# Causal score products of a complex linear-attention kernel: one 128-column product a head against two in 64-column tiles

## The chip, the cores and the metric

The kernel runs on one core of one Trainium2 chip. The metric is the device time of one execution in microseconds (us). The engines are named as in the profile: PE (TensorE, the matrix engine; PEld is its weight loads), DVE (VectorE), ACT (ScalarE), POOL (GpSimd) and SP (the queue that issues most transfers).

## What is computed

The reference is a recurrence over 768 time steps with a state of 48x48 complex numbers for each of 4 batches and 8 heads, and a mixture of experts behind it (cut here to what matters):

```
for t in range(S):                                  # attention
    new_re = ar * S_re - ai * S_im                  # ar, ai: decay of step t, one complex number a channel
    new_im = ar * S_im + ai * S_re
    S_re, S_im = new_re + k[t] v[t]^T, new_im
    y[t] = q[t] S_re
...
x = y of all heads, as rows of 384                  # experts
out[token] = sum over its 2 best of 8 experts of weight * relu(x @ w1[e]) @ w2[e]
```

## The kernel before, in words

The sequence is cut into chunks of 128 steps. A *unit* n is one batch and one chunk, 24 in all (6 chunks of 4 batches), with 8 heads each. Within a chunk the recurrence becomes a matrix product: with queries and keys turned and scaled by the accumulated decay, the output of a chunk is the masked scores times v, plus the queries times the state Z that came from the chunks before.

For a unit the kernel does this, by function and line of the profile:

- `p1`, `p2t`, `p2s`, `p3` (L286 to L344): logarithms, sums over the chunk on PE with a triangular matrix (L307, L331, tile `cum`), sines and exponentials on ACT, products on DVE. These fill `qh` and `kh`, the turned queries and keys.
- `tr_unit` (L354, L355): eight transposes on PE each of `qh` and `kh` into the PSUM tile `ptr`, which ACT copies to `qT` and `kT` (112 rows: 48 real, 16 empty, 48 imaginary).
- `sc_unit` (L363, L364), twice a unit with four heads each (a *half unit*, 48 in all): one product a head, keys as weights (128 columns) against 128 queries, into a quarter of the PSUM tile `psc`, of which there are two. DVE multiplies the four by the causal mask into `am`.
- `st_unit` (L374): 16 products of keys with v into `pG`, 48 columns wide; DVE adds `pG` to the state Z.
- `y_unit` (L412, L414): per head one product with Z and one with `am`, both 48 columns wide, into `pY`: even heads to partitions 0 to 47, odd heads to 64 to 111.
- `x_unit` (L427) and the gate (L436, 32 columns wide; L446; L477, L479) behind it, then scatter of the rows to the experts by POOL.

An fp32 product appears in the trace as two instructions (two passes), a transpose as one. A product of 48 columns in partitions 0 to 63 or 64 to 127 uses one half of the array's columns, and products in the two halves stand in the trace side by side.

What sets the order: a table of names written out by hand (`ORDER`, where P5a/P5b are the two half units of `sc_unit`, P6 `st_unit`, P7a/P7b `y_unit`, D12 the mask) fixes the order on PE, ACT and DVE for the first 17 of the 24 units; a list scheduler places the remaining units together with the first expert's weights (`load_w1`, `load_w2`), the first expert products (`mm1`, L684, which also use `psc`) and the gates. Transfers wait in SP's queue in program order; `load_v` (L267) of a unit stands behind the last reader of the buffer that it takes.

The experts follow (L684 `ph`, L734 `po`), from about 266 us on, and are not touched.

Of the kernel before, what the change touches and what calls it, by code (L numbers as in the profile page):

```python
# [9 lines left out]
F32 = mybir.dt.float32  # L10
# [5 lines left out]
OP = mybir.AluOpType  # L16
# [61 lines left out]
def kernel(  # L78
# [34 lines left out]
    def ones_where(t, cmp, pattern, cm, base, fill):  # L113
        nc.gpsimd.affine_select(out=t, in_=t, pattern=pattern, compare_op=cmp, fill=fill,
                                base=base, channel_multiplier=cm)
# [1 line left out]
    ident = cp.tile([128, 128], F32, name="ident")  # L117
    tri_t = cp.tile([128, 128], F32, name="tri_t")
    tri_l = cp.tile([128, 128], F32, name="tri_l")
    mask = cp.tile([128, 128], F32, name="mask")  # L120
    tri_b = cp.tile([128, 128], BF16, name="tri_b")
    ones_b = cp.tile([128, 128], BF16, name="ones_b")
    nc.vector.memset(tri_t, 1.0 / (2.0 * math.pi))
# [1 line left out]
    nc.vector.memset(tri_l, 0.25)  # L125
    ones_where(tri_l, OP.is_ge, [[1, 128]], -1, 0, -0.25)
    nc.vector.memset(mask, 1.0)
    ones_where(mask, OP.is_ge, [[1, 128]], -1, 0, 0.0)
    make_identity(nc, ident)
    nc.vector.memset(tri_b, 1.0)  # L130
    ones_where(tri_b, OP.is_gt, [[1, 128]], -1, 0, 0.0)
# [53 lines left out]
    nc.vector.memset(pG, 0.0)  # L185
    pY = psA.tile([128, H // 2, 128], F32, name="pY", bufs=1)
    nc.vector.memset(pY, 0.0)


    RE, IM, T0, TH, TF, TR, EE, QK, V = {}, {}, {}, {}, {}, {}, {}, {}, {}  # L190
# [49 lines left out]
    def key(name, ins):  # L240
        K.setdefault(name, []).append(ins)
        return ins
# [20 lines left out]
        nc.sync.dma_start(QK[n], qk[n])  # L263

    def load_v(n):
        V[n] = pa.tile([128, H, D], F32, name="v", bufs=6)
        nc.sync.dma_start(V[n].rearrange("p h d -> p (h d)"), v[n])  # L267

    def flat(t):
# [87 lines left out]
    def sc_unit(n, half):  # L357
        if half == 0:
            AM[n] = pa.tile([128, H, 128], F32, name="am", bufs=2)
        p = psA.tile([128, 4, 128], F32, name="psc")  # L360
        for j in range(4):
            h = 4 * half + j
            key(f"P5{'ab'[half]}.{n}", nc.tensor.matmul(p[:, j, :], KT[n][:, h, :], QT[n][:, h, :], start=True, stop=True))  # L363
        LAST['am'] = nc.vector.tensor_mul(AM[n][:, 4 * half:4 * half + 4, :], p, mask[:, None, :].to_broadcast([128, 4, 128]))  # L364
        key(f"D12{'ab'[half]}.{n}", LAST['am'])

    def st_unit(n):
# [31 lines left out]
    def y_unit(n, half):  # L399

        b, g = bt(n)
        if b == 0 and half == 0:
            XR[g] = pa.tile([128, B, ROW], F32, name="xr", bufs=3)
            nc.gpsimd.memset(XR[g][:, :, RNO + 1:ROW], 0.0)
            nc.gpsimd.tensor_copy(XR[g][:, :, RNO], tokid[:, g])
        for i in (2 * half, 2 * half + 1):
            for z in range(0 if g else 1, 2):
                for r in range(2):
                    h = 2 * i + r
                    o = pY[64 * r:64 * r + D, i, :]  # L410
                    if z == 0:
                        x = nc.tensor.matmul(o, Z[b][:, h, :], QT[n][:, h, :], start=True, stop=False, skip_group_check=True)  # L412
                    else:
                        x = nc.tensor.matmul(o, V[n][:, h, :], AM[n][:, h, :], start=not g, stop=True, skip_group_check=True)  # L414
                    key(f"P7{'ab'[half]}.{n}", x)
        if half == 0:
            return
        XT[n] = pa.tile([128, H // 2, 128], F32, name="xT", bufs=6)
        LAST['y'] = YC[n] = nc.scalar.activation(XT[n], pY, AF.Copy)
        key(f"A13.{n}", YC[n])  # L420
# [92 lines left out]
    def at(step, f, *a):  # L513
        fill.setdefault(step, []).append((f, a))
# [74 lines left out]
    def ps_tile(name, bufs=2):  # L589
        if psB and name == "px":  # L590
            return po_tile()
        if psB:
            return psB[0].tile([128, 512], F32, name=name, bufs=bufs)
        if name == "px":
            return psA.tile([128, H, 128], F32, name="ptr", bufs=1).rearrange("p a b -> p (a b)")[:, 0:512]
        return psA.tile([128, 4, 128], F32, name="psc").rearrange("p a b -> p (a b)")


    order = mybir.DependencyInfo(mybir.DependencyClass.NoSync, mybir.DependencyReason.DATA)
# [126 lines left out]
    def mm2_tile(e, w, j, p=None):  # L726
# [22 lines left out]
        if n == 128 and e in TAILS:  # L749

            for s in DONE.setdefault(e, []):
# [1 line left out]
            DONE[e].append(d)  # L753


    P = dict(la=10, p1=7, d1=1, p2=6, dt=0, ds=0, lqk=6, p3=4, d3=0, q=2, lv=5, xu=0.5, ss=3, gl=0, gd=0.25,
             tr=1.4, sc=-0.2, st=0.05, y=0.2, up=0.4, w1=16.5, w2=21.1, xt=17.8, m1=18.4, dm=0.36, xu1=22.8, w1b=23, co=6, hg=50,
             hx=50, hl=200, s0=(7, 5.5, 4.5), s1=(7.5, 6, 5), qd=0.05, tk=0.4, sh=0.05)
    pri = {gpick: P["hg"], gdis: P["hg"], gscat: P["hg"], x_unit: P["hx"], glog: P["hl"], gturn: P["hl"]}
# [26 lines left out]
            for i in range(2):  # L786
                at(pos(n + .5 - P["q"] + i * P["qd"], f"D{10 + i}.{n}"), p3q, n, i)
    for n in range(NT):
        at(-18.7 + .01 * n if n < 6 else behind_key(n + .5 - P["lv"], f"P7b.{n - 6}"), load_v, n)
        for i in range(2):  # L790
            at(pos(n - P["tr"] + P["tk"] * i, f"P{3 + i}.{n}"), tr_unit, n, i)
        for half in range(2):
# [149 lines left out]
    def slow_attention():  # L942
        with tc.tile_pool(name="sa", bufs=1) as sa, tc.tile_pool(name="sps", bufs=1, space=PSUM) as sps:
# [7 lines left out]
            with tc.For_i(0, NG, 1) as ci, tc.For_i(0, C, 1) as tt:  # L951
# [7 lines left out]
                        nc.sync.dma_start(x[:, 2 + i, b * H:(b + 1) * H],  # L959
                                          a6[bass.ds(ci, 1), bass.ds(tt, 1), i, :, b // 2, b % 2].rearrange("g s d h -> (g s d) h"))  # L960
                vb = sa.tile(sh, F32, name="vb")
                v4 = v.rearrange("(g b) s x -> g s b x", b=B)
                for b in range(B):
                    nc.sync.dma_start(vb[:, b * H:(b + 1) * H, :].rearrange("p h d -> p (h d)"),
                                      v4[bass.ds(ci, 1), bass.ds(tt, 1), b].rearrange("g s x -> (g s) x").to_broadcast([D, HD]))
# [109 lines left out]
def _laid_out(inputs, np):  # L1075

    x = {n: _tiles(np.asarray(inputs[n]), np) for n in ("q", "k", "v", "a_re", "a_im")}
    C, HD = x["q"].shape[1:]
    B = inputs["q"].shape[0]
    a = np.stack([x["a_re"].reshape(-1, 2, C, HD), x["a_im"].reshape(-1, 2, C, HD)], 1)  # L1080
    noise = np.asarray(inputs["moe_noise"])
    E = noise.shape[1]
    laid = dict(inputs, qk=np.stack([x["q"], x["k"]], 2), v=x["v"], a=a.transpose(0, 1, 3, 2, 4),
                moe_noise=noise.reshape(B, -1, C, E).transpose(2, 1, 0, 3).reshape(C, -1, E))
    return {n: laid[n] for n in _INS}

# [21 lines left out]
```

## Time and profile before

| | |
|---|---|
| runs before | 686.52 us median of 3 (686.1 to 687.8) |
| profiled execution | span 685.6 us from the first to the last instruction; the page gives no other time for it, so 0.9 us below the median of the runs |
| attention | the first 266 us; experts from there to the end |
| busy share | PE 94%, PEld 84%, DVE 63%, ACT 48%, POOL 26% |
| score products (L363) | 384 instructions, 53.8 us with at least one running, 5% of the chain of waits |
| mask (L364) | 48 instructions, 32.8 us on DVE |

A busy PE is read with care: matrix products overlap, so what one costs is read from the start of its group to the start of the next group.

### The profile page before, as it was taken

The page shows a single profiled execution, that of the slowest core. Times are in us where ns is not written, and L with a number is a line of the kernel's source. Part 1 is how long each engine was busy: PE and PEld are TensorE (multiplying, and loading weights), DVE is VectorE, ACT ScalarE, POOL GpSimd, SP SyncE. Part 2 cuts the span into 40 slices and gives each one's busy share as a digit, 9 for nine tenths or more (in the row PEclk, how much of TensorE's full clock was granted, in tenths as well). Part 3 has the DMA queues.
Part 4 walks back from the last instruction along what each step waited for, and adds up shares of the span by engine and source line. Part 5 has one row for each costly group of instructions (what it writes and reads, how often), then busy time and mean ns, then how long its engine had stood idle before and what let it go on. Part 6 is the DMA issues. An engine that isn't in the chain of part 4 may idle for free.

```text
span 685.6 us, 13100 instructions
## 1 busy us (share of the span) xinstructions
PE 647.8 (94%) x4982; PEld 577.2 (84%) x4982; DVE 434.3 (63%) x950; ACT 329.6 (48%) x553; POOL 174.9 (26%) x183
## 2 busy tenths in 40 slices
PE   1699999999998999999999999999999999999995
PEld 0378888787777898989898999899899899899995
DVE  7798989898987848546625654744744744734311
ACT  7699888888785444342403512513512612512300
POOL 3000011352412334302422412412412412412311
PEclk9989999999999999999999999999999999999998
DMA  8866855573436455626545453824723743502201
GB/s 306 282 207 202 287 149 168 163 216 95 133 79 222 153 196 188 186 44 163 160 95 168 139 100 104 243 63 145 199 57 101 216 85 116 186 24 69 68 36 34
DMA packets 90397, 100.22 MB, mean 146 GB/s; under 512 B 54554, under 2 KB 74397, under 8 KB 90320
## 3 DMA queue, kind: packets, MB, share of 16 engines
q1 hardware_dynamic: 80960, 71.69, 37.3%
q0 software_dynamic: 9360, 27.54, 11.3%
q8 instruction: 45, 0.74, 0.5%
q14 instruction: 32, 0.26, 0.1%
HBM read 68.55 MB, written 31.69 MB: 146 GB/s over the span
## 4 chain that ended last, share of the span: by engine, by line
PE 84%; DVE 7%; ACT 5%; DMA 2%; issue 1%; SPq 0%; POOL 0%; POOLq 0%; DVEq 0%; ACTq 0%
PE po L734 29%; PE ph L684 29%; PE psc L363 5%; PE ptr L354 4%; PE pY L412 2%; PE pY L414 2%; PE cum L307 2%; PE psc L684 2%; ACT t L248 2%; PE po L740 2%; PE pG L374 2%; PE cum L427 1%; PE cum L331 1%; DVE qk L336 1%; PE cum L436 1%
## 5 line engine op out<-in xcount | busy, mean ns | idle before, releaser
L734 PE MATMUL po<-w2h,h 128*128 128x384 f32 x768 | 196.5, 334 | 0.0
L684 PE MATMUL ph<-x,w1h 128*128 128x512 f32 (+2 forms) x720 | 185.9, 346 | 0.0
L684 PEld LDWEIGHTS ph<-x,w1h 128*128 128x128 f32 x720 | 126.2, 189 | 16.1 <-DVE x L666 0.2
L734 PEld LDWEIGHTS po<-w2h,h 128*128 128x128 f32 x768 | 138.8, 188 | 0.1
L734 PE MATMUL po<-w2l,h 128*128 128x384 f32 x384 | 128.4, 334 | 0.0
L684 PE MATMUL ph<-x,w1l 128*128 128x512 f32 (+2 forms) x360 | 124.6, 346 | 0.0
L746 POOL DMA_INDIRECT out_dram<-ao,ox x52 | 51.2, 985 | 251.5 <-DVE ao L745 232.6
L497 POOL DMA_INDIRECT xs<-xr,sl x48 | 60.9, 1269 | 201.5 <-DMA ecol<-es 92.1
L690 DVE SCALAR_TENSOR_TENSOR h<-ph,h 128x512 fp32r<-128x512 f32 (+2 forms) x144 | 70.1, 504 | 62.6 <-ACT h L686 61.9
L686 ACT ACTIVATE h<-ph 128x512 fp32r<-128x512 f32 (+2 forms) x120 | 60.7, 509 | 97.7 <-PE ph L684 83.3
L745 DVE SCALAR_TENSOR_TENSOR ao<-po,ex,ao 128x384 f32<-128x384 f32 (+1 forms) x42 | 25.9, 616 | 90.0 <-PE po L734 89.8
L607 ACT CAST w2h<-raw 128x768 fp32r<-128x768 f32 x32 | 26.5, 834 | 105.8 <-PE po L734 82.4
L684 PEld LDWEIGHTS ph<-x,w1l 128*128 128x128 f32 x360 | 67.9, 189 | 7.9
L734 PEld LDWEIGHTS po<-w2l,h 128*128 128x128 f32 x384 | 72.1, 188 | 0.1
L709 POOL DMA_INDIRECT ao<-out_dram,ox x49 | 56.6, 1154 | 43.2 <-issue 23.6
L363 PE MATMUL psc<-qT,kT 112*128 112x128 f32 x384 | 53.8, 282 | 1.0 <-ACT kT L355 0.5
L363 PEld LDWEIGHTS psc<-qT,kT 112*128 112x128 f32 x384 | 48.5, 194 | 5.8 <-issue 1.8
L414 PE MATMUL pY<-am,v 128*48 128x128 f32 x384 | 38.5, 275 | 1.9 <-DVE am L364 1.9
L665 ACT CAST x<-xt 128x512 fp32r<-128x512 f32 (+1 forms) x39 | 21.2, 546 | 36.8 <-DVE xt L664 30.9
L364 DVE TENSOR_TENSOR am<-psc,mask 128x512 f32<-128x512 f32 x48 | 32.8, 684 | 8.8 <-PE psc L363 7.7
L608 DVE TENSOR_TENSOR w2l<-raw,w2h 128x768 fp32r<-128x768 f32 x32 | 30.4, 956 | 12.5 <-ACT w2h L607 11.4
L412 PE MATMUL pY<-qT,z 112*48 112x128 f32 x320 | 34.2, 279 | 0.2 <-DVE z L397 0.2
(218 smaller groups left out, 932.5 us busy)
## 6 DMA issues: line engine op xcount, KB each, us to landing
raw<-in_moe_w_dram SPq DMA_DIRECT2D x24, 512.0 KB
raw<-in_moe_w_dram SPq DMA_DIRECT2D x32, 384.0 KB
qk<-in_qk_dram SPq DMA_DIRECT2D x24, 384.0 KB
xgb<-xs SPq DMA_DIRECT2D x28, 192.0 KB
v<-in_v_dram SPq DMA_DIRECT2D x24, 192.0 KB
out_dram<-zero SPq DMA_DIRECT2D x12, 384.0 KB
re<-in_a_dram SPq DMA_DIRECT2D x11, 384.0 KB
im<-in_a_dram SPq DMA_DIRECT2D x11, 384.0 KB
```

What stands on the lines that cost most here:

```text
L363: key(f"P5{'ab'[half]}.{n}", nc.tensor.matmul(p[:, j, :], KT[n][:, h, :], QT[n][:, h, :], start=True, stop=True))
L364: LAST['am'] = nc.vector.tensor_mul(AM[n][:, 4 * half:4 * half + 4, :], p, mask[:, None, :].to_broadcast([128, 4, 128]))
L412: x = nc.tensor.matmul(o, Z[b][:, h, :], QT[n][:, h, :], start=True, stop=False, skip_group_check=True)
L414: x = nc.tensor.matmul(o, V[n][:, h, :], AM[n][:, h, :], start=not g, stop=True, skip_group_check=True)
L497: d = nc.gpsimd.indirect_dma_start(out=xs, out_offset=bass.IndirectOffsetOnAxis(ap=sl[:, kk, b:b + 1], axis=0), in_=XR[g][:, lo + b, :], i ...
L608: d = nc.vector.tensor_tensor(lo, raw_t, hi.bitcast(F32), op=OP.subtract)
L684: LAST['m'] = nc.tensor.matmul(p[:, :c], W1[e, kk][i][:, f * 128:(f + 1) * 128], XW[w, kk][:, j, 0:c], start=(m == 0), stop=(m == len(ms) ...
L686: nc.scalar.activation(h[:, 0:c], p[:, :c], AF.Relu)
L690: LAST['h'] = nc.vector.scalar_tensor_tensor(h[:, dst:dst + b - a], p[:, a:b], 0.0, h[:, a:b].bitcast(F32), op0=OP.max, op1=OP.subtract)
L709: nc.gpsimd.indirect_dma_start(out=ao[j][0:w, :], out_offset=None, in_=out, in_offset=bass.IndirectOffsetOnAxis(ap=OX[e][0:w, j:j + 1], ax ...
L734: LAST['po'] = key(f"PO.{e}.{j}", nc.tensor.matmul(p[:, :DM], HT[w, f][i][:, o:o + 128], W2[f // 2][k2][:, f % 2, :], start=(m == 0), stop ...
L746: d = nc.gpsimd.indirect_dma_start(out=out, out_offset=bass.IndirectOffsetOnAxis(ap=OX[e][0:n, j:j + 1], axis=0), in_=a, in_offset=None, b ...
```

## The change

Keys 0 to 63 of a head meet all 128 queries (64 columns of weights against 128), keys 64 to 127 only queries 64 to 127 (64 against 64); the quadrant of keys 64 to 127 with queries 0 to 63 is not computed. Even heads put their first key half in partitions 0 to 63 and the second in 64 to 127, odd heads the other way round, so that consecutive products lie in different column halves. For odd heads the rows of `am` are therefore swapped by halves; v is laid out by the host with a second, swapped copy of the odd heads (576 columns a row instead of 384), and the mask has a second version. `psc` becomes two fixed tiles, zeroed once; `v` has four buffers instead of six.

```diff
-    mask = cp.tile([128, 128], F32, name="mask")
+    mask = cp.tile([128, 2, 128], F32, name="mask")
...
-    ones_where(mask, OP.is_ge, [[1, 128]], -1, 0, 0.0)
+    ones_where(mask[:, 0], OP.is_ge, [[1, 128]], -1, 0, 0.0)
+    for i in range(2):
+        ones_where(mask[64 * i:64 * i + 64, 1], OP.is_ge, [[1, 128]], -1, 64 * (i - 1), 0.0)
...
+    psc = [psA.tile([128, 4, 128], F32, name=f"psc{i}", bufs=1) for i in range(2)]
+    for t in psc:
+        nc.vector.memset(t, 0.0)
+
+    def next_psc():
+        psc.append(psc.pop(0))
+        return psc[-1]
...
-        V[n] = pa.tile([128, H, D], F32, name="v", bufs=6)
+        V[n] = pa.tile([128, H + H // 2, D], F32, name="v", bufs=4)
...
-        p = psA.tile([128, 4, 128], F32, name="psc")
-        for j in range(4):
-            h = 4 * half + j
-            key(f"P5{'ab'[half]}.{n}", nc.tensor.matmul(p[:, j, :], KT[n][:, h, :], QT[n][:, h, :], start=True, stop=True))
-        LAST['am'] = nc.vector.tensor_mul(AM[n][:, 4 * half:4 * half + 4, :], p, mask[:, None, :].to_broadcast([128, 4, 128]))
+        p = next_psc()
+        for s, js in ((0, (0, 1, 2, 3)), (64, (1, 0, 3, 2))):
+            for j in js:
+                h = 4 * half + j
+                o = 64 * (h % 2) if s == 0 else 64 * (1 - h % 2)
+                key(f"P5{'ab'[half]}.{n}", nc.tensor.matmul(p[o:o + 64, j, s:], KT[n][:, h, s:s + 64], QT[n][:, h, s:],
+                                                            start=True, stop=True, skip_group_check=True))
+        LAST['am'] = nc.vector.tensor_mul(AM[n][:, 4 * half:4 * half + 4, :].rearrange("p (i r) t -> p i r t", r=2),
+                                          p.rearrange("p (i r) t -> p i r t", r=2),
+                                          mask[:, None].to_broadcast([128, 2, 2, 128]))
...
-                        x = nc.tensor.matmul(o, V[n][:, h, :], AM[n][:, h, :], start=not g, stop=True, skip_group_check=True)
+                        x = nc.tensor.matmul(o, V[n][:, H + i if r else h, :], AM[n][:, h, :], start=not g, stop=True, skip_group_check=True)
...
-    P = dict(la=10, p1=7, d1=1, p2=6, dt=0, ds=0, lqk=6, p3=4, d3=0, q=2, lv=5, xu=0.5, ss=3, gl=0, gd=0.25,
+    P = dict(la=10, p1=7, d1=1, p2=6, dt=0, ds=0, lqk=6, p3=4, d3=0, q=2, lv=3, xu=0.5, ss=3, gl=0, gd=0.25,
...
-        at(-18.7 + .01 * n if n < 6 else behind_key(n + .5 - P["lv"], f"P7b.{n - 6}"), load_v, n)
+        at(-18.7 + .01 * n if n < 4 else behind_key(n + .5 - P["lv"], f"P7b.{n - 4}"), load_v, n)
```

How the change moves instructions is seen at three places.

PE, in the part whose order the table fixes (unit 6 here; `kh`, `qh` with their buffer numbers, `pG`, `ptr` and `cum` as above). Before:

```order
L427 MATMUL cum<-ident,xT 128x128 x4
L363 MATMUL psc<-qT,kT 128x128 x4
L374 MATMUL pG<-v,kh_126 48x48 x16
L354 MATMUL ptr<-ident,qh_125 112x128 x8
L363 MATMUL psc<-qT,kT 128x128 x4
L331 MATMUL cum<-t_638,tri_l 128x384
L354 MATMUL ptr<-ident,kh_127 112x128 x8
```

The same place in the changed kernel, whose lines are numbered 9 to 14 higher:

```order
L441 MATMUL cum<-ident,xT 128x128 x4
L374 MATMUL psc_144<-qT,kT 64x128 x4
L374 MATMUL psc_144<-qT,kT 64x64 x4
L388 MATMUL pG<-v,kh_128 48x48 x16
L363 MATMUL ptr<-ident,qh_127 112x128 x8
L374 MATMUL psc_145<-qT,kT 64x128 x4
L374 MATMUL psc_145<-qT,kT 64x64 x4
L340 MATMUL cum<-t_658,tri_l 128x384
L363 MATMUL ptr<-ident,kh_129 112x128 x8
```

The first number of a shape is the width in columns. A run of score products was 128 columns wide and is now 64 wide; everything around it stands where it stood. Up to the tri_t products of the last chunk the orders of the two kernels differ in nothing else on PE.

PE, in the part that the scheduler orders (a half unit of one of the last units, beside the gate and the turning of the first expert's rows, `ptr<-ident,xga`). Before:

```order
L363 MATMUL psc<-qT,kT 128x128 x2
L427 MATMUL cum<-ident,xT 128x128
L436 MATMUL cum<-xT,wg 32x128 x12
L427 MATMUL cum<-ident,xT 128x128 x2
L659 MATMUL ptr<-ident,xga 128x128
L427 MATMUL cum<-ident,xT 128x128
L446 MATMUL cum<-ident,lt 128x96
L659 MATMUL ptr<-ident,xga 128x128 x2
L363 MATMUL psc<-qT,kT 128x128 x6
```

In the changed kernel:

```order
L374 MATMUL psc_145<-qT,kT 64x128
L441 MATMUL cum<-ident,xT 128x128 x8
L374 MATMUL psc_145<-qT,kT 64x128 x2
L450 MATMUL cum<-xT,wg 32x128 x12
L673 MATMUL ptr<-ident,xga 128x128 x3
L374 MATMUL psc_145<-qT,kT 64x128
L460 MATMUL cum<-ident,lt 128x96
L374 MATMUL psc_145<-qT,kT 64x64 x4
```

The half unit is now cut into four pieces, where it was cut into two.

DVE, at the very start (`t` the tiles of `p1`; `bad<-bad` at L893 adds two guard values that ACT accumulates beside its second and fourth instruction; ISA is the two-part reduction of L287). Before:

```order
L187 MEMSET pY 128x512
L286 TENSOR_TENSOR t_203<-im,t_202 128x384
L287 ISA t_202,bad<-t_203 128x384
L287 ISA bad 128x1
L286 TENSOR_TENSOR t_203<-im,t_202 128x384
L289 SCALAR_TENSOR_TENSOR t_201<-t_201,t_202 128x384
L287 ISA t_202,bad<-t_203 128x384
L287 ISA bad 128x1
L893 TENSOR_TENSOR bad<-bad 128x1
```

In the changed kernel:

```order
L189 MEMSET pY 128x512
L192 MEMSET psc_144 128x512
L192 MEMSET psc_145 128x512
L295 TENSOR_TENSOR t_205<-im,t_204 128x384
L907 TENSOR_TENSOR bad<-bad 128x1
L296 ISA t_204,bad<-t_205 128x384
L296 ISA bad 128x1
L295 TENSOR_TENSOR t_205<-im,t_204 128x384
L298 SCALAR_TENSOR_TENSOR t_203<-t_203,t_204 128x384
```

Two memsets came in, and the small addition `bad<-bad`, which stood behind both reductions, now stands ahead of the first.

SP's queue keeps its order in the part that the table fixes; in the last chunk the v loads of the last two units stand behind some of the `ecol` transfers and the first expert weights, where all v loads preceded these before.

## Rows read from the trace of the kernel before

**Rows 1.** The page, part 1: busy us (share of the span) xinstructions

```profile
PE 647.8 (94%) x4982; PEld 577.2 (84%) x4982; DVE 434.3 (63%) x950; ACT 329.6 (48%) x553; POOL 174.9 (26%) x183
```

**Rows 2.** Busy time by stretch, (x) instructions, in two stretches of the attention

```profile
core 0: us, PE busy (x) PEld busy (x) DVE busy (x) ACT busy (x) POOL busy (x), PEclk, DMA share, GB/s
86.00:103.00 17.00, 17.00 (x223) 14.43 (x222) 15.20 (x47) 15.12 (x30) 2.77 (x2) 1.00 0.55 147
103.00:120.00 17.00, 17.00 (x204) 13.73 (x203) 17.00 (x30) 14.51 (x21) 2.92 (x2) 1.00 0.54 166
```

**Rows 3.** The chain of waits by line, from 43 to 160 us, then 160 to 183

```profile
by line: PE psc L363 18.5%; PE ptr L354 16.0%; PE cum L307 8.7%; PE pY L412 8.7%; PE pY L414 8.3%; PE pG L374 7.9%; PE cum L331 6.2%; PE cum L427 4.9%; PE cum L436 2.6%; ACT t L248 2.3%; ACT ee L248 1.9%; DVE kh L344 1.6%; DVE am L364 1.5%;
...
by line: DVE qk L336 15.3%; DVE kh L344 12.1%; ACT t L248 11.3%; DVE t L286 8.0%; DVE am L364 7.8%; DVE t L287 7.6%; ACT kT L355 4.1%; DVE z L381 4.0%; DVE qh L344 3.8%; DVE t L291 3.8%; DVE t L289 3.8%; issue 3.2%; DVE ga4ix L59 1.8%; ACT 
```

**Rows 4.** PE's timeline around 160 us: start us, us, what, count [idle before]

```profile
157.64 0.92 PE L374 MATMUL pG<-v,kh 128*48 128x48 f32 x32
158.49 1.16 PE L363 MATMUL psc<-qT,kT 112*128 112x128 f32 x8
159.49 0.81 PE L331 MATMUL cum<-t,tri_l 128*128 128x384 f32 x2
160.13 1.05 PE L363 MATMUL psc<-qT,kT 112*128 112x128 f32 x8
161.12 0.42 PE L412 MATMUL pY<-qT,z 112*48 112x128 f32 x4
...
162.41 0.39 PE L414 MATMUL pY<-am,v 128*48 128x128 f32 x4
162.63 0.89 PE L374 MATMUL pG<-v,kh 128*48 128x48 f32 x32
163.44 1.08 PE L354 MATMUL ptr<-ident,kh 128*112 128x128 f32 x8
164.46 0.43 PE L412 MATMUL pY<-qT,z 112*48 112x128 f32 x4
164.71 0.39 PE L414 MATMUL pY<-am,v 128*48 128x128 f32 x4
...
165.16 0.39 PE L414 MATMUL pY<-am,v 128*48 128x128 f32 x4
165.47 0.91 PE L331 MATMUL cum<-t,tri_l 128*128 128x384 f32 x2
166.22 1.06 PE L363 MATMUL psc<-qT,kT 112*128 112x128 f32 x8
167.12 0.81 PE L331 MATMUL cum<-t,tri_l 128*128 128x384 f32 x2
```

**Rows 5.** PE's timeline: a group of transposes between neighbours as wide

```profile
94.69 1.04 PE L354 MATMUL ptr<-ident,qh 128*112 128x128 f32 x8
95.57 0.17 PE L479 MATMUL cum<-ohs,tri_b 128*128 128x8 bf16 x1
```

**Rows 6.** Groups by line: the mask product on DVE (busy us, mean ns | idle before, releaser)

```profile
L364 DVE TENSOR_TENSOR am<-psc,mask 128x512 f32<-128x512 f32 x48 | 32.8, 684 | 8.8 <-PE psc L363 7.7
```

**Rows 7.** DVE's timeline at the start

```profile
2.80 0.48 DVE L187 MEMSET pY<- 128x512 f32 x1
4.44 0.56 DVE L286 TENSOR_TENSOR t<-im,t 128x384 f32<-128x384 f32 x1 [1.16 <-ACT t L248]
5.03 0.56 DVE L287 CUSTOM_DVE_ANT_0 t<-t 128x384 f32<-128x384 f32 x1
```

**Rows 8.** ACT's timeline at the start and at 32.6 us

```profile
6.85 0.19 ACT L248 ACTIVATION_READ_ACCUMULATOR t<-t 128x1 f32 x1
6.94 0.51 ACT L248 ACTIVATE t<-t 128x384 f32<-128x384 f32 x1
...
32.60 0.49 ACT L248 ACTIVATE ee<-cum 128x384 f32<-128x384 f32 x1 [1.16 <-DMA es<-ee]
```

**Rows 9.** SP's timeline: the first v loads

```profile
12.75 2.80 SPq L267 DMA_DIRECT2D v<-in_v_dram  x6
```

More of the change, by code (lines that the diff above doesn't have):

```diff
@@ L595, in ps_tile @@
             return psA.tile([128, H, 128], F32, name="ptr", bufs=1).rearrange("p a b -> p (a b)")[:, 0:512]
-        return psA.tile([128, 4, 128], F32, name="psc").rearrange("p a b -> p (a b)")
+        return next_psc().rearrange("p a b -> p (a b)")
     order = mybir.DependencyInfo(mybir.DependencyClass.NoSync, mybir.DependencyReason.DATA)
@@ L961, in slow_attention @@
                 vb = sa.tile(sh, F32, name="vb")
-                v4 = v.rearrange("(g b) s x -> g s b x", b=B)
+                v4 = v[:, :, 0:HD].rearrange("(g b) s x -> g s b x", b=B)
                 for b in range(B):
@@ L1078, in _laid_out @@
     C, HD = x["q"].shape[1:]
-    B = inputs["q"].shape[0]
+    B, H = inputs["q"].shape[:2]
     a = np.stack([x["a_re"].reshape(-1, 2, C, HD), x["a_im"].reshape(-1, 2, C, HD)], 1)
@@ L1082, in _laid_out @@
     E = noise.shape[1]
-    laid = dict(inputs, qk=np.stack([x["q"], x["k"]], 2), v=x["v"], a=a.transpose(0, 1, 3, 2, 4),
+    odd = np.roll(x["v"].reshape(-1, C, H // 2, 2, HD // H)[:, :, :, 1], C // 2, axis=1)
+    laid = dict(inputs, qk=np.stack([x["q"], x["k"]], 2), a=a.transpose(0, 1, 3, 2, 4),
+                v=np.concatenate([x["v"], odd.reshape(-1, C, HD // 2)], 2),
                 moe_noise=noise.reshape(B, -1, C, E).transpose(2, 1, 0, 3).reshape(C, -1, E))
```

## The prediction

> **What bounds the kernel now.** I read the shares first: PE is busy 94% of the span [rows 1]. Shares mix stages, so the busy time by stretch comes next: in the attention PE is busy all of 86 to 103 and of 103 to 120 us, and DVE is busy 15.2 and 17.0 of the same 17 us [rows 2]. So PE is the engine to relieve there, with DVE close behind. The chain of waits tells which of the two sets the end: from 43 to 160 us nearly all of it is PE, the score products alone 18.5% of 117 us, or 21.6 us; some 27 half units of about 0.96 us run there, so four in five of their microseconds lie on the chain. From 160 to 183 us the chain is DVE and ACT, and no score product of weight is in it [rows 3]. The last view is PE's timeline, which has the prices: a group costs the time from its start to the next group's start.
>
> **The change part by part.** All sums are made against the profiled execution (span 685.6 us); the median of the runs is 0.9 us above it, and I carry differences over to 686.5.
>
> *Score products.* Between neighbours of its own width a half unit takes 0.90 us for eight instructions (166.22 to 167.12), 0.11 each [rows 4]. Four pY instructions, of two heads in the two column halves, take 0.22 us (162.41 to 162.63): a pair in both halves costs the 0.11 of one wide instruction [rows 4]. pG, with 48 columns against 48, takes 0.81 us for 32 instructions, 0.09 of it for leaving the halves (priced below): 0.72 over 16 pairs is 0.045 a pair [rows 4]. The new half unit has four pairs of 64 columns against 128 and four of 64 against 64. The first four cost 4 x 0.11 = 0.44. The second four are not in the trace; they lie between the 48-wide pair, 0.045, and the pair that streams 128, 0.11, so 0.18 to 0.44. I take 0.06 a pair, 64/48 of the first, to which they are nearest: 0.24. A half unit is then 0.68 instead of 0.90 (0.62 to 0.88), and 48 of them save 48 x 0.22 = 10.6 us of PE.
>
> *Changes of width.* They eat most of that. A half unit that is followed by pY takes 0.99 instead of 0.90 (160.13 to 161.12), and the first pY group after such a change 0.25 instead of 0.22 (164.46 to 164.71): going into the halves costs 0.12 to 0.13 [rows 4]. Out of them, the last pY group takes 0.31 instead of 0.22 (165.16 to 165.47), and the group that follows pays again because its first weights load in the open: score products 1.00 for 0.90 (158.49 to 159.49), a triangular product 0.75 for 0.64 (165.47 to 166.22, against 159.49 to 160.13) [rows 4]. Eight transposes take 1.02 less the 0.09 of the change behind them, 0.93, for 0.88 [rows 4, 5]. So out costs 0.14 to 0.20, 0.17 on average. The Trainium skill, "TensorEngine Tiling (Array Packing)", Key Properties, says that changing the tiling mode drains TensorE, and its Overview, Theoretical Speedup, promises up to 2x for columns up to 64; by the speedup alone the sum would be -10.6 us, by the drain it is what follows, and the trace shows the drain.
>
> Score products were 128 wide among many 128-wide neighbours. Counted along PE's order up to the experts, the program goes into the halves 59 times before and 85 times after, and out 59 and 84 times; 27 of the 55 runs of score products now stand alone between 128-wide work (there 0.22 is saved and 0.12 + 0.17 paid, a loss), and only 21 touch 64-wide work on one or both sides. That is 26 x 0.13 + 25 x 0.17 = 7.6 us. The changes to and from the 32-wide gate products stay at 14.
>
> *By part.* In the part that the table orders (36 half units, up to about 190 us) there are 34 more changes: -36 x 0.22 + 17 x 0.30 = -2.8 us. In the scheduler's part (12 half units) there are 17 more, and half units are cut so that more products stand alone in one half: -2.6 + 2.6 = 0, at worst half a microsecond more.
>
> *What reaches the end.* Of the 2.8 us some 2.2 fall before 160 us, on the chain; what falls under the DVE and ACT stretch of 160 to 183 us is worth nothing, the rest before 190 us about 0.2. I take **-2.4 us**, between 0 (DVE takes over) and -2.8.
>
> *The start.* The three memsets grow by 2 x 0.48 and some 0.1 us; DVE then idles 1.16 us for ACT [rows 7], which covers them by a tenth. The addition bad<-bad is dearer. It needs the second value that ACT accumulates, there at 6.85 + 0.19 = 7.04 us [rows 8], and now holds the first reduction, which ran at 5.03 [rows 7]. ACT's logarithm at 6.94 [rows 8] waits for that reduction (0.56), so it starts no sooner than 7.6, or 0.7 to 0.9 us late with the addition itself, and everything that ACT and DVE do up to 17 us moves with it. What hides it: at 32.60 us ACT idles 1.16 us for a transfer of SP's queue [rows 8]. SP's loads of the decay at 12 us wait for the same ACT work and would be late too, but behind them stand six v loads of 2.80/6 = 0.47 us each [rows 9], now four: SP is back in step. If that cover holds the cost is 0, if not 0.9; I take **+0.2**.
>
> *Off the path.* The mask product keeps its 512 columns, 0.684 us [rows 6]; its operands are only addressed in one dimension more. v grows by half (24 x 96 KB), in the same first 1152 KB and then loads four units ahead, near 9 us each, instead of six; that lead is the cover, and only a lead under one unit would cost. The last two v loads now make expert weights wait behind an output four units back, which is done by then. Two mask fillings on POOL lie beside its other work at the start.
>
> Sum: -2.4 + 0.2 = -2.2 us, so a span of 683.4 and a median of **684.3 us**. A measurement of this kernel can tell about 0.3% (2.1 us) from no change, so this stands at the edge, 684.4.
>
> **The rivals.**
>
> 1. *Slower: the tail's cut half units.* From 190 us on the scheduler interleaves single score products with gate products and turns of rows; five runs are broken off and finished later. A mask cannot start before its last product, so each broken half unit puts a mask (0.684) and one pair of changes (0.30) in front of waiting pY products: 5 x 0.98 = 4.9 us, 689.2. It decides from 4.3 us of new waiting on PE in the tail. For it: the tail has broken runs already. Against: PE has other work there, and the broken runs before are of the same kind. Chance 0.16.
> 2. *No change: DVE takes over.* DVE had no idle time from 103 to 120 us [rows 2]; if its queue sets the pace PE only waits more, and the start stays: 686.7. Against: DVE is idle 1.8 us from 86 to 103 [rows 2], and its waits for score products, 7.7 us in all [rows 6], get shorter. Chance 0.20.
> 3. *Slower: weight loads of the halves one after the other.* If two loads of 64 columns did not run side by side, the half unit would stay near 0.90, nothing would be saved, and the 7.6 us of changes, four fifths of them on the chain, would give 692.8. Against: pG's pairs, each with two loads, take 0.045 us [rows 4], and a pair of 48-wide loads behind one another would have to fit there. Chance 0.03. The Trainium skill, "TensorE: Matmul & The Clock Gate", LDWEIGHTS, gives columns/1.2 ns a load, 53 ns for 64 columns; sixteen in a row would be 0.85 us, this rival's case, which pG's rows speak against.
> 4. *Faster: the changes cost less around score products* (the change of width would then be pY's and pG's own matter), or the scheduler's new tail is shorter: -10.6 x 0.8 = -8.5 us at the most, 678.0. Against: the score products themselves showed the 0.10 on both sides [rows 4]. Chance 0.06.
>
> **How the numbers follow.** The forecast has 0.55, its own range 682.8 to 686.0: 0.34 of it below 684.4, 0.21 within. Faster: 0.34 + 0.06 = 0.40. Same: 0.21 + 0.20 = 0.41. Slower: 0.16 + 0.03 = 0.19. The range reaches from 681.5 (the second four pairs at 0.045 and both ends of the start and of the chain in favour: 48 x 0.06 x 0.8 = 2.3 us more) to 689.2 (rival 1); rivals 3 and 4 stay out.
>
> **What would show it.** In the changed profile a half unit between 64-wide neighbours takes 0.68 us, one between 128-wide neighbours 0.68 + 0.13 and its follower 0.05 to 0.11 more; the mask still takes 0.684. The first reduction starts past 7.1 us, and ACT's wait at 32.6 us is shorter by as much. PE's work up to 190 us is some 2.8 us shorter. I am wrong if 64-against-64 pairs take 0.11, if PE waits for masks more than 4 us longer in the tail, or if PE stands idle for DVE between 43 and 160 us.

## The result, and the profile after

| | before | after |
|---|---|---|
| first comparison, median (runs) | 686.85 us (686.1 to 687.8) | 692.17 us (691.08 to 693.97) |
| ratio | | 1.0075, 95% interval 1.006 to 1.009 |
| profiled execution | span 685.6 us | 691.08 us, span 689.3 us |

The change makes the kernel slower; it had been forecast 0.3% faster. The profiled execution after is the fastest of its four, so the traces show 3.7 of the 5.3 us between the medians. Six chips served in what follows. The kernel before takes 686.9 us on the first (A) and 687.9 on another (D), 681.4 to 682.0 on the other four (B, C, E, F). So each kernel is compared with before on its own chip.

The profile after, with the views of before beside it. The page's first part, against [rows 1]:

```profile
PE 648.6 (94%) x5366; PEld 569.8 (83%) x5366; DVE 434.8 (63%) x952; ACT 330.2 (48%) x553; POOL 175.2 (25%) x185
```

There are 384 more matrix instructions, and PE is as busy as before. PE's timeline has the prices, against [rows 4]: a half unit between wide neighbours (first two rows), and one between pY groups:

```profile
50.94 0.89 PE L374 MATMUL psc<-qT,kT 112*64 112x128 f32 x16
51.76 1.08 PE L363 MATMUL ptr<-ident,qh 128*112 128x128 f32 x8
...
110.90 0.84 PE L374 MATMUL psc<-qT,kT 112*64 112x128 f32 x16
111.57 0.39 PE L426 MATMUL pY<-qT,z 112*48 112x128 f32 x4
```

From start to next start that is 0.82 us between wide neighbours and 0.67 between pY groups; 0.81 and 0.68 had been forecast. The sizes of the new products were right. The mask still takes 0.684 us. That the saving does not become time shows in the busy times by stretch, against [rows 2]:

```profile
core 0: us, PE busy (x) PEld busy (x) DVE busy (x) ACT busy (x) POOL busy (x), PEclk, DMA share, GB/s
86.00:103.00 17.00, 17.00 (x248) 13.36 (x248) 15.70 (x47) 15.05 (x30) 2.77 (x2) 1.00 0.67 211
103.00:120.00 17.00, 15.69 (x211) 12.09 (x205) 15.94 (x29) 13.75 (x21) 3.35 (x2) 1.00 0.56 164
```

From 103 to 120 us PE, which had been busy all the time, now stands for 1.3 us. Its waits in that stretch, and then DVE's (us in all, times, longest):

```profile
PE pY L426 <- DVE z L411: 0.9, 1, 0.9
PE cum L316 <- issue: 0.3, 1, 0.3
```

```profile
DVE fcol L405 <- DMA ecol<-es: 0.9, 1, 0.9
```

So here PE waited 0.9 us for the state z, which DVE could not scale because `ecol` was late: the decay at the chunk's last step, which goes out to memory (`es`) and comes back as a column. The other 0.3 us is a gap with no wait that the profile shows. Both are of the changed kernel and of this chip, and both come back below; the waits for DVE's work as such are read on another chip. From 86 to 103 us transfers went from 147 to 211 GB/s.

### The profile page after: what moved, and what is told of

It is laid out like the page before. It is cut to its first block, busy times and chain, and to the rows that moved or that the text cites. A ratio compares the mean times of both kernels' runs of the same rounds, so it can differ in the third digit from the quotient of the medians.

```text
span 689.3 us, 13880 instructions
## 1 busy us (share of the span) xinstructions
PE 648.6 (94%) x5366; PEld 569.8 (83%) x5366; DVE 434.8 (63%) x952; ACT 330.2 (48%) x553; POOL 175.2 (25%) x185
## 4 chain that ended last, share of the span: by engine, by line
PE 77%; DVE 10%; ACT 4%; DMA 3%; issue 2%; another core or an unknown queue 2%; SPq 1%; POOL 0%; DVEq 0%; POOLq 0%; ACTq 0%
PE ph L698 28%; PE po L748 28%; PE psc L374 4%; PE ptr L363 4%; PE cum L316 2%; PE pY L428 2%; PE pY L426 2%; DMA es<-ee 2%; PE psc L698 2%; PE cum L441 1%; PE po L754 1%; ACT t L257 1%; PE pG L388 1%; PE cum L340 1%
## 5 line engine op out<-in xcount | busy, mean ns | idle before, releaser
L374 PEld LDWEIGHTS psc<-qT,kT 112*64 112x64 f32 x768 | 38.3, 138 | 14.6 <-issue 10.1
L374 PE MATMUL psc<-qT,kT 112*64 112x128 f32 (+1 forms) x768 | 46.2, 256 | 2.6 <-DVE sl L503 1.2
```

What stands on the lines that cost most here:

```text
L374: key(f"P5{'ab'[half]}.{n}", nc.tensor.matmul(p[o:o + 64, j, s:], KT[n][:, h, s:s + 64], QT[n][:, h, s:], start=True, stop=True, skip_grou ...
```

## The experiments

**Parts of the change.** e1 to e4 keep everything around the products (v of 576 columns, psc, mask) and choose by unit and half which product is used (y_unit takes the swapped copy of v only with the new product):

```diff
+    def new(n, half):
+        return False                      # e1;  n < 17: e2;  n >= 17: e3;  a list of 13 half units: e4
...
-        for s, js in ((0, (0, 1, 2, 3)), (64, (1, 0, 3, 2))):
+        if new(n, half):
+            for s, js in ((0, (0, 1, 2, 3)), (64, (1, 0, 3, 2))):
...
+        else:
+            for j in range(4):
+                h = 4 * half + j
+                key(f"P5{'ab'[half]}.{n}", nc.tensor.matmul(p[:, j, :], KT[n][:, h, :], QT[n][:, h, :], ...
```

e1: 

> All that surrounds the change is kept (v of 576 columns in four buffers, the second mask, psc as two fixed tiles), but every half unit is the old 128-column product again. PE's order up to 195 us is that of before, behind it nearly so. Theory A (the loss lies in the products themselves, their changes of width and their order): as before, 686.9, at most 0.5 off. Rival E (the surroundings cost: 2.4 MB more to read, v loads two units later, two more memsets and an addition moved ahead at the start): 688 or more.

e2: 

> New products in the units 0 to 16 (the order written by hand), old ones in the last seven units; PE's order in the tail is that of e1. Theory T (most of the loss is made behind 190 us: another order of the scheduler, the clock that falls at 267 us, a late first expert): the changed kernel's PE was 0.5 us behind the old one at 190 us and 4.4 behind at 290, so about 687.5, 4 to 5 below the changed kernel. Rival S (PE's dense stretches from 108 us on carry the loss): 691 to 692, no better than the changed kernel. The forecast's own account of the table part, -2.8 on PE, would give 684.5.

e3: 

> The complement: old products in the units 0 to 16, new ones in the last seven; PE's order is that of the changed kernel everywhere. Theory T: 690.5 to 691.5, nearly all of the changed kernel's loss. Rival S: about 687, the tail is neutral as the forecast had it.

e4: 

> New products only in the 13 of the 34 half units of the table that stand beside a 64-wide group (pG or pY) on at least one side; old ones elsewhere and in the tail. By the prices of the forecast each saves 0.22 and adds no change of width, and one loses a pair of changes (0.30): 13 x 0.22 + 0.30 = 3.2 us of PE. Theory W (what a product gives is eaten by changes of width, the rest reaches the end): 684.0 to 684.8. Rival D (the saving ends in waits for DVE and in PE's own stalls from 108 us on): 686 to 687.

Measured on chip B (before 681.89): e1 1.0033 (1.0021 to 1.0044), e2 1.0043 (1.0029 to 1.0057), e3 1.0025 (1.0014 to 1.0035), e4 1.0047 (1.003 to 1.0064). The surroundings alone cost 0.33%, 2.1 us (rival E). Beside that the products hardly matter: in the table +0.7 us, in the tail -0.5, both inside the intervals. Theory T, that most of the loss is made in the tail's products, fails with e3. e4 kept only the half units that were cheapest by my prices, 3.2 us of PE, and is no faster than e1: W fails. That does not rest on the median alone, for in e4's profiled execution the clock fell in the tail, to 0.50 from 220.76 us on for 3.41 us; up to 190 us, ahead of that, it gained some 0.5 us (table below).

**The changed kernel on other chips, and two pieces of the surroundings.** c_after and d_after are the changed kernel, c_before the kernel before, for its trace. e5 and f4 put the addition of bad back behind the reduction; e6 is e1 with the v of before; f3 is e6 with four buffers:

```diff
+        tc.add_manual_dep(x.ins, K[f"D2b.{m}"][-1].ins.name, after, reason="behind the reduction")   # e5, f4
...
-        V[n] = pa.tile([128, H + H // 2, D], F32, name="v", bufs=4)
+        V[n] = pa.tile([128, H, D], F32, name="v", bufs=6)                                          # e6, f4;  bufs=4 in f3
```

c_after: 

> The changed kernel again, beside the others on one chip. From e1 (1.0033), e2 (1.0043) and e3 (1.0025), if surroundings, table and tail add up: 1.0033 + 0.0010 - 0.0008 = 1.0035 of the kernel before. If the two parts make each other worse (stalls of the table that only count with the new tail, a clock that falls): 1.0075, as in the first comparison.

c_before: 

> The kernel before again, for a trace from the same chip: where e1 to e4 lose their 1.6 to 3 us is to be read against it. At the start its first reduction does not wait for ACT's second sum.

e5: 

> The changed kernel, with the one-column addition of bad held behind the second half's reduction, where the kernel before has it. Theory A (the start costs nothing in the end, what it loses is covered by 34 us): as the changed kernel. Rival B (the start's 0.7 to 0.9 us reach the end): 0.5 to 0.9 us below the changed kernel, 0.1%.

e6: 

> e1 (old products everywhere) with the v of before too: 384 columns, six buffers, loads six units ahead. What remains of the surroundings is the second mask, two fixed psc tiles with their memsets, and the addition moved ahead at the start; PE's order is that of before. Theory V (v's loads, later and half as large again, and the other order that they give the scheduler, cost e1's 2.1 us): 1.000 to 1.001 of before. Rival P (psc and the start cost it): 1.003.

d_after: 

> The changed kernel as a control on this chip. Theory S (PE's supply of instructions gives out on some chips): 1.003 if the kernel before takes 681 to 682 here, 1.007 if it takes 686 to 688, with 3 to 4 us of PE gaps without a wait in that case and none in the other. Rival (the first difference was the spread of its four runs): 1.003 to 1.005 on either kind of chip.

f3: 

> e6 (old products, v of 384 columns) with four buffers of v and loads four units ahead as in the changed kernel. PE's order is that of before but for seven groups. Theory O (v costs by its 576 columns, which make the scheduler order the tail otherwise): as e6, 1.001. Rival L (late loads cost it): as e1, 1.003.

f4: 

> e6 with the addition of bad held behind the reduction, as in the kernel before: of the surroundings only the larger memsets, the second mask and the fixed psc tiles stay. Theory A (the addition costs e6's 0.7 us): 1.000. Rival M (the memsets, or psc as fixed tiles): 1.001.

Measured on chip C (before 681.37): c_after 1.0031 (1.0019 to 1.0042), e5 1.0029 (1.0016 to 1.0041), e6 1.0012 (1.0003 to 1.002). On chip E (before 681.37): d_after 1.0045 (1.0032 to 1.0058), f3 1.0039 (1.0026 to 1.0052), f4 1.0000 (0.9991 to 1.0009). So the memsets, the second mask and psc cost nothing that shows. c_after is what the pieces add up to (1.0035), in part by luck, since its loss is not made of the same waits as e1's (below). d_after, on another chip as quick, has 1.0045 and no gaps; theory S's other half, the changed kernel on a slow chip other than A, was not run. The addition costs up to 0.8 us (e6 against f4, on two chips, whose intervals overlap), though holding it back in the changed kernel gave only 0.1 (e5: its theory A, though B's 0.5 to 0.9 lies inside the intervals). Four buffers instead of six cost 1.8 us (f3 against e6, on two chips, both with the addition ahead: 1.0039 and 1.0012); theory O, that the 576 columns are to blame, fails.

The start, DVE's timeline of e6 and then of f4:

```profile
4.50 0.56 DVE L295 TENSOR_TENSOR t<-im,t 128x384 f32<-128x384 f32 x1
6.97 0.16 DVE L916 TENSOR_TENSOR bad<-bad 128x1 f32<-128x1 f32 x1 [1.91 <-ACT t L257]
7.05 0.55 DVE L296 CUSTOM_DVE_ANT_0 t<-t 128x384 f32<-128x384 f32 x1
```

```profile
4.50 0.56 DVE L295 TENSOR_TENSOR t<-im,t 128x384 f32<-128x384 f32 x1
5.09 0.56 DVE L296 CUSTOM_DVE_ANT_0 t<-t 128x384 f32<-128x384 f32 x1
```

With the addition ahead the reduction starts at 7.05 instead of 5.09 us, as forecast. For v, f3 shows the path. SP's queue, then ACT's casts of the first expert's weights, then PE:

```profile
207.25 0.35 SPq L276 DMA_DIRECT2D v<-in_v_dram  x1
209.19 2.42 SPq L639 DMA_DIRECT2D raw<-in_moe_w_dram  x3
217.35 0.33 SPq L276 DMA_DIRECT2D v<-in_v_dram  x1
217.78 2.18 SPq L647 DMA_DIRECT2D raw<-in_moe_w_dram  x2
...
221.05 1.04 ACT L630 CAST w1h<-raw 128x1024 fp32r<-128x1024 f32 x1 [2.25 <-DMA raw<-in_moe_w_dram]
...
222.15 0.56 PE L707 MATMUL psc<-x,w1h 128*128 128x320 f32 x2 [1.87 <-ACT w1h L630]
```

The same cast in f4, where the last v load is issued at 196.88 us:

```profile
196.88 0.33 SPq L276 DMA_DIRECT2D v<-in_v_dram  x1
208.46 2.22 SPq L639 DMA_DIRECT2D raw<-in_moe_w_dram  x3
...
217.88 1.04 ACT L630 CAST w1h<-raw 128x1024 fp32r<-128x1024 f32 x1
```

With four buffers two more v loads stand in SP's queue, each waiting for a pY product, and the weights behind them come later; PE stands 1.87 us for a cast. Every kernel with four buffers and the old products in the tail has the same wait: e1 1.2 us, e2 0.9, e4 1.7. c_after has not: its new order in the tail does not need that cast so early.

**Who sets the pace.** The start of the same instruction, a product into qh or kh on DVE (the 7th, the 21st and the 39th), and of PE's first po product, in us later than in c_before; the span likewise. Each row is one execution, and B, E and F have no trace of the kernel before (it takes within 0.1% of C's time there):

```
              42.3   102.9   189.7   first po   span
f4           +1.00   +1.00   +0.86    +0.86     +0.5
e6           +1.42   +1.41   +1.28    +1.31     +1.1
f3           +0.96   +0.95   +0.83    +3.25     +4.1
e1           +1.32   +1.33   +1.21    +3.14     +2.7
e2           +2.63   +2.40   +2.34    +3.93     +3.3
e3           +1.56   +1.56   +1.82    +2.56     +2.3
e4           +1.13   +0.76   +0.59    +4.89     +4.0
c_after      +0.30   +0.06   +0.12    +0.87     +1.3
e5           +0.47   +0.22   +1.95    +2.68     +2.3
f1           +2.40   +2.16   +2.84    +3.84     +4.3
d_after      +1.61   +1.37   +3.78    +4.77     +5.4
g1           +2.13   +4.20   +5.87    +5.91     +5.1
g2           +0.53   +2.92   +7.21    +7.27     +6.9
before (A)   +0.83   +0.83   +2.15    +6.61     +6.3
after (A)    -0.10   -0.34   +2.59    +8.21    +10.0
```

A lag at 42 us is still there at 190: kernels with old products take back 0.1 of it, those with new ones in the table (e2, e4, c_after) 0.2 to 0.5. (In d_after a late transfer and a fall of the clock at 113 us come in between, in e3, e5 and f1 a late transfer; both below.) From 43 to 190 us, c_after against c_before: PE's idle time grows from 1.87 to 3.52 us, while the end of the stretch comes 0.2 (by DVE's instruction in the table above) to 0.4 us earlier (by pG groups on PE, from the one at 48.8 to the one at 188.7 us). So about 2 us of PE's work went (the forecast had 2.8 for all 36 half units, two of them ahead of 42 us), and nearly all of it became idle time. Part of that, 0.4 us, is the late ecol; but in e2 and e4, where ecol is in time and the saving is as small, PE's waits of over 0.15 us from 43 to 190 us are all for DVE but one of 0.5 us for ACT. The busy times from 103 to 160 us in c_before and in c_after:

```profile
103.00:160.00 57.00, 56.90 (x718) 46.63 (x708) 53.90 (x115) 49.53 (x76) 23.32 (x16) 1.00 0.58 178
```

```profile
103.00:160.00 57.00, 55.92 (x830) 44.06 (x820) 53.69 (x115) 49.40 (x76) 20.07 (x16) 1.00 0.62 189
```

PE lost 1 us of work, DVE next to none: it is busy 94% of the stretch. Whether its last 6% are room is not to be read from a share. Three kinds of experiment bear on it. r1 moves a piece of DVE's work to POOL, e8 and g1 add to DVE, g2 adds to PE:

```diff
-            key(f"D15.{n}", nc.vector.tensor_mul(Z[b], Z[b], FC[g]...
+            key(f"D15.{n}", nc.gpsimd.tensor_mul(Z[b], Z[b], FC[g]...           # r1_before, r1_after
...
+        if 4 <= n < 16:
+            key(f"D9.{n}", nc.vector.tensor_copy(junk, QK[n][:, 0, 0:360]))     # e8 (changed), g1 (before)
...
-        for j in range(4):
+        for j in (0, 1, 2, 0, 1, 2, 3) if half == 0 and 4 <= n < 16 else range(4):   # g2 (before)
```

r1_before: 

> The kernel before with DVE relieved: the scaling of the state (z times decay, D15, 20 products of 112x384, 0.55 us each on DVE) is done by POOL, which is idle for most of the attention. In the table 16 of them leave DVE, 8.8 us. Theory D (DVE, not PE, sets the pace from 43 to 190 us): faster by some of this, 1 to 4 us, as far as POOL is not late itself. Rival P (PE sets it): within 0.5 us of before.

r1_after: 

> The changed kernel with the same relief. Theory D: with DVE out of the way PE's saving of 1.8 us in the table shows, so the relief is worth 1 to 2 us more here than in the kernel before: the ratio falls from 1.003 below that of the relieved kernel before plus 0.0005. Rival P: 1.003, as the changed kernel. If POOL is late with z both lose, and what is left to compare is only their difference.

e8: 

> The changed kernel with one copy of 128x360 more on DVE in each of the units 4 to 15, 0.3 to 0.5 us each, 12 in all, 3.6 to 6 us; PE's order is that of the changed kernel. Theory D: PE's pace follows DVE's, the drift at 190 us grows by 60% or more of what the copies take, so 685 to 689 on a chip that gives the kernel before 681.5. Rival P: PE goes on as before, 684, and DVE's idle time swallows the copies.

g1: 

> The kernel before with a copy of 128x360 more on DVE (0.347 us, measured in e8) in each of the units 4 to 15, 4.16 us in all; the order is that of before. Theory D (DVE sets the pace): 3 to 4.2 us slower, all of it by 160 us. Rival P (PE sets it, DVE has slack): under 1 us.

g2: 

> The kernel before with three of the score products issued twice in the first half unit of the units 4 to 15, 3 x 0.11 = 0.33 us of PE each, 4.0 us in all. Theory D alone (PE only fills its waits): under 1 us. Rival P: 3 to 4 us. Both engines at their limit, so that adding to either costs and taking from one gives nothing: 2 to 4 us here and in g1.

Measured on chip D (before 687.85): r1_before 1.004 (1.0023 to 1.0057), r1_after 1.0122 (1.0098 to 1.0147), e8 1.0167 (1.0147 to 1.0186). On chip F (before 681.99): g1 1.0055 (1.004 to 1.007), g2 1.01 (1.0083 to 1.0117). The relief failed: on POOL the scaling takes 0.83 to 2.9 us instead of 0.55, and PE waits 1.1 us for z by 190 us; it decides nothing. Its trace shows one thing all the same: DVE ran ahead (its 39th product into qh or kh starts at 187.5 us, against 191.8 in before on A) and PE did not (143.7 us from its third pG group to its 17th, against 143.5). e8 lost more than its copies explain by themselves, on a chip where PE has gaps of its own (below) and where the changed kernel was not run; it decides nothing either.

g1 and g2 decide. g1's copies are 4.16 us on DVE and cost 3.6, or 88%; seven of them, 2.43 us, lie ahead of the instruction at 102.9 us, and the lag grows by 2.07 from 42.3 us up to there. g2's products cost 6.5 us. There my expectation had a slip: a wide product is two instructions of 0.11, so three are 0.67 us, not 0.33, and twelve pieces 8.0; 6.5 is 81% of it. So D alone and P alone both fail. Both engines are at their limit: adding to either costs most of it, and taking from one alone, as the change does, gives a fifth or less. How the two hold each other shows in the waits for the mask product between the scores and y. PE's wait for it in g1, 43 to 195 us (in c_before 0.3 up to 190):

```profile
PE pY L417 <- DVE am L367: 2.3, 4, 0.8
```

and DVE's wait for the scores in g2, 43 to 195 us (in c_before 2.3):

```profile
DVE am L364 <- PE psc L363: 5.5, 9, 1.1
```

DVE stood idle 8.7 of the 147 us from 43 to 190 in c_before, more than g1 added, and yet g1's copies cost nearly all they took: that idle time was no room.

**The other losses.** f1 gives the seven half units beside a pG the old product; e7 puts v in two tiles, five buffers of 384 columns and two of 192:

```diff
+        return (n, half) not in ((0, 1), (6, 0), (10, 0), (10, 1), (12, 1), (13, 0), (14, 0))       # f1
...
+        VO[n] = pa.tile([128, H // 2, D], F32, name="vo", bufs=2)                                  # e7
+        nc.sync.dma_start(VO[n].rearrange("p h d -> p (h d)"), v[n][:, HD:])
```

f1: 

> The changed kernel, but the seven half units of the table that stand directly beside a pG (units 0b, 6a, 10a, 10b, 12b, 13a, 14a) take the old products, which halves PE's instructions there. PE's order stays. These seven lose a saving of 0.22 each and some changes of width, 1.5 to 2 us of PE. Theory S: where the gaps exist, those near 122, 144 and 160 us go away, 1.5 us, and the time falls by 0 to 1.5 us; where they don't exist, the time stays (DVE sets the pace). Rival W (PE sets the pace): 1 to 2 us slower than the changed kernel.

e7: 

> The changed kernel with v in two tiles: the natural 384 columns in five buffers, loaded five units ahead, the swapped 192 of the odd heads in two; the same bytes, 24 transfers more. Theory V (v's late loads and what the scheduler makes of them cost 1.4 us): 1.0 to 1.5 us below the changed kernel, ratio 1.001. Rival L (the scheduler's order is a lottery, any other transfer reshuffles the tail): anywhere from 1.000 to 1.006, with the part up to 190 us unchanged.

Measured: f1 on chip E 1.0021 (1.0011 to 1.0031), 1.6 us below d_after on the same chip, though only 0.7 below c_after's ratio, which is inside the intervals; PE alone does not set the pace (W fails). Neither trace on E has gaps without a wait, so S does not explain the gain, and it stays open. e7 on chip D 1.0144 (1.0113 to 1.0176): V fails in this form, and so does L, which had at most 1.006. What e7 is worse by than the changed kernel is not known, since D has no run of that.

Gaps on PE are the likeliest extra loss on chips A and D, where the change costs more: 0.75% on A (0.31 and 0.45 on C and E), and 0.8% on D from r1_before to r1_after. No run took the gaps away. PE around 121 us after the change on chip A, then on chip C:

```profile
119.71 0.89 PE L374 MATMUL psc<-qT,kT 112*64 112x128 f32 x16
120.43 0.89 PE L388 MATMUL pG<-v,kh 128*48 128x48 f32 x32
121.58 0.60 PE L374 MATMUL psc<-qT,kT 112*64 112x128 f32 x6 [0.26 <-issue]
122.33 0.42 PE L374 MATMUL psc<-qT,kT 112*64 112x128 f32 x4 [0.16 <-issue]
123.06 0.39 PE L374 MATMUL psc<-qT,kT 112*64 112x64 f32 x6 [0.31 <-issue]
123.39 0.91 PE L340 MATMUL cum<-t,tri_l 128*128 128x384 f32 x2
```

```profile
120.30 0.89 PE L388 MATMUL pG<-v,kh 128*48 128x48 f32 x32
121.02 0.86 PE L374 MATMUL psc<-qT,kT 112*64 112x128 f32 x16
121.80 0.91 PE L340 MATMUL cum<-t,tri_l 128*128 128x384 f32 x2
```

"issue" is time in which PE waited for nothing that the profile shows. After the change there are eleven such gaps of over 0.15 us, 4.3 us in all; e7 and e8 have 4.6 and 4.1, r1_after 2.2; before and r1_before have one of 0.45 and 0.38. The fourteen profiles from chips B, C, E and F have none. Seven of the eleven lie in groups of psc or pG, where short instructions stand together, some 0.73 us apart. By the Trainium skill, "Runtime: NRT & Kernel Launch", Instruction fetch mechanics, fetching instructions is hidden behind their issue; the four chips agree, and on the two others that is the suspect, which no run here showed. The pages do not tell it either: the instruction transfers of queue 8 are as many on A as on C (48, 0.79 MB).

Two more things cost new kernels now and then. DVE waits at 109 us for ecol: 0.4 to 2.0 us in eight of the nine profiles with the tail's new products (in e7, the longest, another transfer is named), in none of the others. From e5's row above it can be most of what a run loses: 1.7 us more lag from 103 to 190 us, behind a wait of 1.56. In d_after it is

```profile
111.22 0.19 DVE L405 TENSOR_TENSOR fcol<-ecol,ecol 112x32 f32<-112x32 f32 x1 [1.72 <-issue]
```

And in the tail the scheduler now puts the last gate behind a turn of rows. PE after the change on chip A:

```profile
264.42 0.38 PE L673 MATMUL ptr<-ident,xga 128*128 128x128 f32 x1 [0.76 <-DVE x L680]
...
266.96 0.24 PE L460 MATMUL cum<-ident,lt 32*128 32x32 f32 x1 [0.62 <-DVE x L680]
```

Busy time and granted clock (PEclk) around it:

```profile
262.00:267.20 5.20, 3.67 (x35) 2.61 (x31) 4.33 (x25) 4.43 (x10) 0.00 (x0) 1.00 0.00 0
267.20:270.61 3.41, 3.41 (x12) 3.41 (x13) 3.13 (x10) 1.29 (x3) 0.00 (x0) 0.50 0.73 202
```

PE stood 1.5 of 5.2 us, and for the next 3.41 us it was granted 0.50, 1.2 GHz. (d_after's fall at 113 us came behind a wait of PE of 1.75 us for z.) From the first po product to the first ph product the lag grows by 1.3 us here, by 1.2 in d_after and f1, which have the fall too, and by 0.1 in c_after, e3 and e5, which have not.

## Why the prediction was wrong

- *Score products and changes of width*: right in their prices, 0.82 and 0.67 us a half unit. PE's work from 43 to 190 us fell by about 2 us, where 34 half units had 2.6 by the forecast; the group behind a new half unit pays 0.04 to 0.19 more (c_after against c_before), not 0.05 to 0.11.
- *What reaches the end* ("Of the 2.8 us some 2.2 fall before 160 us, on the chain"): this is the step that failed. The chain of waits named PE at most of its steps [rows 3], and I took that for room behind PE. DVE held the pace beside it: 4.16 us added to DVE cost 3.6 (g1), 8.0 added to PE cost 6.5 (g2), and 2 us taken from PE gave 0.2 to 0.4. So the term was -2.4 and is -0.2 to -0.4. In [rows 2] DVE's 17.00 of 17 us stood there; rival 2 had the mechanism and the right stretch, and got 0.20.
- *The start*: +0.2 forecast, 0.1 to 0.8 measured (e5; e6 against f4). The first reduction moved as forecast. A lag at 42 us does stay to 190, but the table does not show that the start's own survives the cover at 32.6 us: f4, without the addition ahead, is 1.00 late at 42 us and c_after, with it, 0.30. On chip A the start came out 0.9 us early, since the second half of the decay was there earlier (ACT's logarithm of it at 4.60 us, before at 5.86): that hid the term in the first comparison.
- *Off the path, v*: "an output four units back, which is done by then" failed. The queue is what counts: with old products, four buffers cost 1.8 us through the weights. In the changed kernel this wait is not there, so of its own loss this is not shown to be a part.
- *The tail* was taken at 0, and e3 against e1 (-0.5 us) seems to say so; but e1's tail has the wait for the cast. From 190 us to the first po product f4 and e6, which have neither, lose 0.0 us, and the five traces with the changed order on chips B, C and E 0.7 to 1.0: a wait of 0.81 us ahead of the last gate, with or without the fall of the clock behind it. Rival 1's cut half units are not what costs: PE's waits for masks in the tail are 0.6 us in c_after and 0.8 in c_before.
- On chip C, where PE has no gaps and the clock did not fall behind the last gate, the spans differ by +1.3 us where -2.2 was forecast: start +0.3, 42 to 190 us -0.2, from there to the first po +0.7, behind it +0.4. So 2.2 of the 3.5 us missed are the step that failed. The medians there differ by 2.3 us; c_after's profiled execution is 1.3 us below its median, and what the other executions lose more is in no trace of it (e5's late ecol shows one way).
- The first comparison from these pieces, A's spans, 3.7 us: start -0.9, 42 to 190 us +1.4 (2.69 of new lag against 1.32 before; 1.8 us of gaps and the late ecol lie in it), from there to the first po +1.2, and behind it +2.0 (1.3 the clock, 0.7 a gap at 284.8 us).

Open stay: what causes the gaps on chips A and D and what they cost in all, why ecol is late with the tail's new products (on no engine does the order ahead of 109 us differ between e2 and the changed kernel), and what f1 gained. No version ran faster than the kernel before.

## What to carry to other kernels

Where a second engine is busy 90% of a stretch, a chain of waits that names the first does not say that a saving there becomes time, and the second's idle share does not say how much of it will: here 8.7 us of idle time took up 0.5 of 4.16 us of added work. A known piece of work added once to each engine tells more than either. A change that halves buffers moves transfers in a queue, and what to look at is not who needs the buffer but who stands behind it in that queue. Here narrow products paid only between narrow neighbours: 0.67 us there for 0.90, but 0.82 among wide ones for 0.89, with 0.04 to 0.19 more on the group behind.

## What was not expected of the hardware

The same kernel differs by 6 us between chips (681.4 to 687.9), and a program with more, shorter PE instructions has up to 4.6 us of PE gaps without a wait on the slower ones. A stand of PE of 0.8 and 0.6 us within 3 us was followed by 3.41 us at half the granted clock in some executions (after, d_after, f1) and in others not (c_after, e3, e5, with the same two waits), and cost 1.2 to 1.3 us each time.
